# A polysketch attention and its expert router on one core: a new order for the steps ahead of the first expert block, and earlier waits at the close

## The chip, the core and the metric

The kernel runs on 1 core of a Trainium2 chip. The metric is the device time of one execution in microseconds (us): the runs shown of the kernel before are 196.06, 192.71 and 194.74 us, with a median of 194.74. All arithmetic on the matrix engine is in fp32, which the program writes as one matmul; the trace shows each such matmul as two or more passes, so counts of PE in the profile are larger than counts in the program.

## The reference

```python
# attention: 4 batches, 4 heads, 1088 rows, 32 columns, r = 8
def phi(x):
    a = np.einsum('rd,bhsd->bhsr', S1, x)
    b = np.einsum('rd,bhsd->bhsr', S2, x)
    return np.einsum('bhsi,bhsj->bhsij', a, b).reshape(*x.shape[:-1], r * r)
q_p, k_p = phi(q), phi(k)
kv = np.einsum('bhsf,bhsd->bhfd', k_p, v)
z = np.sum(k_p, axis=2)
num = np.einsum('bhsf,bhfd->bhsd', q_p, kv)
den = np.einsum('bhsf,bhf->bhs', q_p, z)[..., None] + 1e-06
x = (num / den)          # then heads side by side: 4352 rows of 128
# router: 8 experts, 128 -> 1024 -> 128
xn = x / (np.linalg.norm(x, axis=-1, keepdims=True) + 1e-06)
en = expert_emb / (np.linalg.norm(expert_emb, axis=-1, keepdims=True) + 1e-06)
logits = xn @ en.T / tau
expert_idx = np.argmax(logits, axis=1)
gate_w = softmax(logits)[np.arange(N), expert_idx]
for e in range(8):
    mask = expert_idx == e
    h = np.maximum(x[mask] @ w1[e], 0.0)
    out[mask] = gate_w[mask, None] * (h @ w2[e])
```

Every row goes through one expert alone, so the rows have to be sorted by expert before the two layers can run as full blocks.

## The kernel before, in words

**Two halves.** The four batches are worked on as two groups, `m = 0` and `m = 1`, of two batches each, and each group as five pieces: four of 4 tiles of 128 rows (called 0 to 3) and a rest (called r). For a piece, the keys go through these steps, which carry a name in the tables below (`keys`, L490): `ktr`, four transposes of 128x128 on PE, whose result ACT copies to `kT` (L426, L430); `kab`, the sketch with S1 and S2 together, PE's L447; `kb`, ACT's copy of the second factor (L453); `kp`, the product of the two factors on DVE or POOL (L463); `kv`, the sum of keys times values in PSUM (L529). In the first group a name has a 0 behind the kind (`ktr0 2`), in the second it has none (`ktr 2`). The queries of the first group take another way: `qtr` (L426), `pairs` (L611, 32 passes into two banks that hold both factors already spread), `sec` (ACT copies one factor, L620) and `prod` (DVE's product `held`, L623). Those of the second group go like the keys and are then turned: `trqp` (L641), `qpT` (ACT's copy, L647 or L650). When all keys and values of a group are in, `total` copies the sum to `kz`, `trkv` and `kvT` turn it (L544, L548), and `kve` and `kz` append its product with the experts' embeddings, `en_blk`. Then `nd` (L663) multiplies the queries' features with `kz`, which gives numerator, denominator and router logits at once, and `x` divides, so that the piece's rows and logits are in `xg`.

**Constants ahead of it.** `words` (L208) takes S1 and S2 apart on DVE, `sketches` (L229) turns them on PE (L231) into `Sblk` and `S_pairs`. The experts' embeddings go through `norm emb` (L359: square on ACT, power on POOL), `scale emb` (L367: DVE), `turn emb` (L382: PE's L385) and `place emb` (L387: DVE's `en_blk`). `lane`, `lanes`, `downs`, `positions` and `clear` make tables for the sorting. PE starts with matmuls on zeros that are used by nothing (L112, L115).

**The sorting of the first group.** `best 0`, `place 0`, `count`, `take 0`, `split 0`, `rest`, `mark`, `find`, `sums` and `tokens` find the best expert of each row, count rows by expert and make lists of rows; `exp0` also issues the first block's first layer, `weights(0)` (SP, L1080), whose expert SP reads from a register (L1073). `fetch` gathers a block's rows from DRAM by an indirect DMA of POOL's queue (L1046); `fetch0` is block 0's, `fetch 1` the next ones'. `turn 0` turns block 0's rows (PE's L1056, ACT's copy to `xTb`, L1058).

**The expert blocks.** 35 blocks of 128 rows follow. `up` is 16 passes (L1122) into `ps_big`, ACT's relu (L1130) makes `hT`, `down` is 16 passes (L1158) with the second layer in `w_sb`, and y goes out by an indirect DMA of POOL's queue (L1171). All second layers are loaded ahead of the blocks: six experts' on SP's queue after the keys, queries and values, and the last two in step `best 0` (L188). Group 1's other pieces of `nd` run between the first blocks. At the end SP drains and waits for the last nine first-layer loads (L1301 and L1302).

**What sets the order.** The program is recorded step by step, and each engine executes its instructions in the order of recording; nothing reorders them. Up to block 0 that order is two lists of step names written out by hand, `HEAD` (L399) and `ORDER` (L407). A step records its instructions for all of its engines at once, so a place in the list is a place on PE, ACT, DVE, POOL and the DMA queues of SP and ACT. From block 0 on, a table of times (`put_at`, `in_ticks`) sets the order.

```python
    for i, name in enumerate(x.strip() for x in HEAD.split(";")):
        put_at(0)(0, i, steps[name])
    ...
    for i, name in enumerate(x.strip() for x in ORDER.split(";")):
        put_at(4)(0, 47.2 + 0.01 * i, steps[name])
    put_at(first)(0, 32, lambda: weights(1))
    ...
            for i in sorted(at):
                for _, _, f in sorted(at[i], key=lambda x: x[:2]):
                    f()
```

Of the kernel before, what the change touches and what calls it, by code (L numbers as in the profile page):

```python
# [72 lines left out]
def kernel(  # L73
# [33 lines left out]
    nc.vector.memset(zeros, 0.0)  # L107
    ps_warm = ps_one("acc")

    def keep_warm(n):  # L110
        for _ in range(n):
            nc.tensor.matmul(ps_warm[:, :P], zeros[:, :P], zeros[:, :P], start=True, stop=True)  # L112

    for _ in range(7):
        nc.tensor.matmul(ps_warm[:2 * R, :2 * R], zeros[:, :2 * R], zeros[:, :2 * R], start=True, stop=True)  # L115
# [6 lines left out]
    for i, (s, queue) in enumerate(((S1, nc.sync), (S2, nc.scalar))):  # L122
        queue.dma_start(swords[i * R:(i + 1) * R].rearrange("p d w -> p (d w)"), s.bitcast(U32))
# [284 lines left out]
total0; kab 0 ab; trkv0; kvT0; ktr 1; kb 0; kve0; ktr 3; kz0; kp 0; nd 0 0; kab 1 acc; kb 1; ktr 2; x 0 0; nd 0 1; kp 1; kab 3 ab; kb 3;
kab 2 acc; kb 2; x 0 1; nd 0 2; trqp0r; ktr r; kp 3; kp 2; x 0 2; nd 0 3; kab r ab; kb r; kp r; x 0 3; qtr 1; qtr 0; kv 0; kv 1;
qab 0 t; qb 0; kv 3; best 0; place 0; count; qtr 3; qtr r; qp 0;  # L410
take 0; kv 2; kv r; qtr 2; trqp 0; total; split 0; trkv; qab 1 t; qab 3 ab; rest; mark 00; qb 1;
qab r ab; mark 01; find; exp0; kvT; qab 2 acc; sums; kve; qb 2; qpT 0; qb 3; qb r; qp 1; tokens; qp 3; kz;
trqp 1; nd 1 0; fetch0; fetch 1; qp 2; qp r; x 1 0; trqp 3; qpT 1; others; qpT 3; nd 1 1; x 1 1; trqp 2; norm 0; turn 0;
qpT 2; trqp r; qpT r"""
# [646 lines left out]

    def spread(i):

        squares[i] = tc.dram_tile([4, P // 4, 4, BLOCK], F32, name=f"squares{i}")
        nc.sync.dma_start(squares[i].rearrange("c b j a -> (b j) c a"), xs[i][:, :DM].rearrange("p (c a) -> p c a", c=4))

    def gather_squares(i):
        xq[i] = held[:, 0, i % 4 * P:(i % 4 + 1) * P]
        nc.sync.dma_start(xq[i], squares.pop(i).rearrange("c b j a -> (c b) (j a)"))
# [5 lines left out]

    loads = []
# [74 lines left out]

    def down(i):
# [12 lines left out]
        if i == USUAL - 1:  # L1165
            nc.vector.tensor_scalar_mul(y, ps, gate.pop(i)[:, 0:1])
        else:
            nc.scalar.activation(y, ps, ACT.Copy, scale=gate.pop(i)[:, 0:1])  # L1168
# [31 lines left out]
    def together(*fs):  # L1200
# [4 lines left out]
                  "best 0": together(steps["best 0"], steps["pick 0"], steps["write 0"], lambda: [load_w2(e) for e in (E - 2, E - 1)]),  # L1205
# [96 lines left out]
    for load in loads[-9:]:  # L1302
# [32 lines left out]
```

## Time and profile before

| what | number |
|---|---|
| three runs | 196.06, 192.71, 194.74 us |
| median | 194.74 us |
| the profiled execution | 194.15 us |
| its span from first to last instruction | 192.2 us |
| mean granted clock of PE | 0.994 |
| PE busy | 184.8 us (96%) in 2501 passes |
| weight loads beside it (PEld) | 175.4 us (91%) |
| DVE, ACT, POOL busy | 90.3, 98.7, 103.7 us |
| HBM read and written | 34.69 MB, 6.10 MB |
| block 0's first matmul | at 52.62 us |
| PE's last matmul ends | at about 187.5 us |

The span has three parts: the steps up to block 0 (0 to 52.62 us), the blocks (to 187.5 us), and the close (to 192.2 us). A row of the timeline or the chain gives the start in the span and the length; a releaser in brackets says which engine ended the wait ahead of the row. A row of the table by stages gives each engine's busy time in that stretch with the number of its instructions. Times lie within one profiled execution; the run's own time is 1.95 us longer than its span.

### The profile page before, as it was taken

To read this page: it belongs to the slowest core of one execution; us is meant where nothing else is said; L and a number is where in the kernel's file an instruction comes from. 1 tells how busy PE (TensorE), PEld (TensorE's weight loads), DVE (VectorE), ACT (ScalarE), POOL (GpSimd) and SP (SyncE) were. 2 spreads that over 40 slices of the span, in tenths; PEclk is the share of its full clock that TensorE was granted. 3 is DMA by queue.
4 is the path that set the end of the run, shared out by engine and by line. 5 is a ranking of instruction groups with operands and counts; after the bars stand their busy time and mean duration, and the time that the engine had idled before them with its cause. 6 is when DMAs were issued, how large, how long until landed. Compare 5 with 4: busy or idle time off the path is not lost.

```text
span 192.2 us, 6854 instructions
## 1 busy us (share of the span) xinstructions
PE 184.8 (96%) x2501; PEld 175.4 (91%) x2501; DVE 90.3 (47%) x396; ACT 98.7 (51%) x284; POOL 103.7 (54%) x134
## 2 busy tenths in 40 slices
PE   7999899999999999999999999999999999999990
PEld 7777788989889999999999999999999999999990
DVE  5789767789939578952232122122122121132200
ACT  3575353346572556534565555555555557657430
POOL 5110019302763765577877776776777775740532
PEclk9999999999999999999999999999999999999997
DMA  4999799998394987645558878788768998796000
GB/s 129 333 274 274 186 283 296 270 325 216 113 294 170 306 301 245 195 134 158 120 144 257 213 205 259 194 225 247 193 183 194 271 306 250 222 322 180 31 27 29
DMA packets 42596, 41.18 MB, mean 214 GB/s; under 512 B 17626, under 2 KB 36067, under 8 KB 42563
## 3 DMA queue, kind: packets, MB, share of 16 engines
q1 hardware_dynamic: 40272, 36.06, 64.7%
q0 software_dynamic: 2240, 4.67, 8.4%
q8 instruction: 21, 0.34, 0.8%
q14 instruction: 13, 0.10, 0.2%
q10 hardware_dynamic: 50, 0.01, 0.0%
HBM read 34.69 MB, written 6.10 MB: 212 GB/s over the span
## 4 chain that ended last, share of the span: by engine, by line
PE 70%; DMA 13%; issue 7%; POOL 4%; DVE 3%; ACT 1%; POOLq 1%; ACTq 0%
PE ps_big L1122 23%; DMA out_dram<-y,dst_i 13%; PE ps_acc L1158 11%; PE ps_ab L1158 10%; PE ps_big L663 6%; PE ps_acc L529 4%; PE ps_t L426 3%; POOL xs L1046 3%; PE ps_big L611 2%; PE ps_ab L447 2%; POOL norm L1136 2%; PE ps_acc L112 1%; PE ps_t L854 1%; PE ps_t L1056 1%; DVE row L778 1%
## 5 line engine op out<-in xcount | busy, mean ns | idle before, releaser
L1122 PE MATMUL ps_big<-xTb,wb 128*128 128x128 f32 x512 | 62.7, 276 | 0.4 <-PE ps_big L663 0.3
L1122 PEld LDWEIGHTS ps_big<-xTb,wb 128*128 128x128 f32 x512 | 59.7, 192 | 0.9 <-ACT sq L1135 0.4
L1171 POOL DMA_INDIRECT out_dram<-y,dst_i x35 | 35.9, 1027 | 40.5 <-ACT y L1168 17.6
L1130 ACT ACTIVATE hT<-ps_big 128x1024 f32<-128x1024 f32 x35 | 35.8, 1023 | 40.2 <-PE ps_big L1122 38.8
L1046 POOL DMA_INDIRECT xs<-rows,dst_i x35 | 35.6, 1018 | 18.4 <-DVE dst_i L871 11.4
L1158 PE MATMUL ps_ab<-w_sb,hT 128*128 x272 | 33.6, 276 | 0.0
L1158 PEld LDWEIGHTS ps_ab<-w_sb,hT 128*128 128x128 f32 x272 | 31.7, 192 | 0.2
L1158 PE MATMUL ps_acc<-w_sb,hT 128*128 x240 | 29.2, 275 | 0.0
L1149 DVE TENSOR_SCALAR gate<-gate 128x1 f32<-128x1 f32 x35 | 5.3, 150 | 50.3 <-ACT probs L1146 49.7
L1158 PEld LDWEIGHTS ps_acc<-w_sb,hT 128*128 128x128 f32 x240 | 28.0, 192 | 0.0
L1136 POOL TENSOR_TENSOR norm<-norm,half_c 128x1 f32<-128x1 f32 x35 | 21.7, 621 | 1.7 <-ACT sq L1135 1.3
L1053 DVE STREAM_TRANSPOSE xTb<-held 128x128 f32<-128x128 f32 x22 | 9.1, 413 | 13.6 <-DMA held<-squares 13.5
L463 POOL TENSOR_TENSOR kp<-both 128x1024 f32<-128x1024 f32 (+1 forms) x3 | 4.5, 1512 | 16.4 <-ACT both L458 16.4
L1168 ACT ACTIVATE y<-ps_ab,gate 128x128 f32<-128x128 f32 x17 | 6.2, 367 | 9.4 <-PE ps_ab L1158 9.4
L1146 ACT ACTIVATE probs<-xs,norm 128x8 f32<-128x8 f32 x35 | 10.4, 296 | 1.3 <-DVE norm L1139 1.3
L1168 ACT ACTIVATE y<-ps_acc,gate 128x128 f32<-128x128 f32 x17 | 6.2, 366 | 8.6 <-PE ps_acc L1158 6.8
L1135 ACT ACTIVATE sq<-xs 128x128 f32<-128x128 f32 x35 | 10.6, 302 | 0.1
L529 PE MATMUL ps_acc<-v,kp 128*64 128x64 f32 x224 | 7.8, 224 | 0.6 <-issue 0.6
L529 PEld LDWEIGHTS ps_acc<-v,kp 128*64 128x64 f32 x224 | 7.1, 138 | 1.4 <-issue 1.4
L430 ACT COPY qT<-ps_t 128x512 f32<-128x512 f32 (+1 forms) x10 | 5.1, 534 | 4.3 <-PE ps_t L426 4.3
L1127 PEld LDWEIGHTS ps_big<-xTb,wb 128*64 128x64 f32 x96 | 6.6, 137 | 0.5 <-DVE gate L1150 0.4
L1127 PE MATMUL ps_big<-xTb,v 128*64 128x96 f32 (+1 forms) x96 | 7.0, 249 | 0.0
(279 smaller groups left out, 280.8 us busy)
## 6 DMA issues: line engine op xcount, KB each, us to landing
wb<-in_moe_w_dram SPq DMA_DIRECT2D x35, 512.0 KB
w_sb<-in_moe_w_dram SPq DMA_DIRECT2D x16, 256.0 KB
rows<-xg SPq DMA_DIRECT2D x4, 544.0 KB
v<-in_v_dram SPq DMA_DIRECT2D x4, 512.0 KB
k<-in_k_dram SPq DMA_DIRECT2D x3, 512.0 KB
q<-in_q_dram SPq DMA_DIRECT2D x3, 512.0 KB
v<-in_moe_w_dram SPq DMA_DIRECT2D x3, 512.0 KB
squares<-xs SPq DMA_DIRECT2D x22, 64.0 KB
```

The lines of the kernel that those rows point to most:

```text
L529: nc.tensor.matmul(acc[m][u * HALF:(u + 1) * HALF, i, p], s["kp"][:, c - c0, h], bass.AP(tensor=vo.tensor, offset=vo.offset, ap=[list(vo.a ...
L663: nc.tensor.matmul(ps[i * HALF:(i + 1) * HALF, j * NEXT + p * W:j * NEXT + (p + 1) * W], q_[:, p, k_ * P + i * HALF:k_ * P + (i + 1) * HAL ...
L1046: nc.gpsimd.indirect_dma_start(out=xs[i][:], out_offset=None, in_=rows[:2 * S if t == 0 else N + 1], in_offset=bass.IndirectOffsetOnAxis(a ...
L1122: nc.tensor.matmul(ps[:, u, j * P:(j + 1) * P], w[:, f * P:(f + 1) * P], x, start=True, stop=True)
L1127: nc.tensor.matmul(ps[r, u, j * P + n0:j * P + n1], (w, first_b(i))[b][:, f * P + c * HALF:f * P + (c + 1) * HALF], x[:, n0:n1], start=Tru ...
L1130: nc.scalar.activation(hT[i], ps, ACT.Relu)
L1135: nc.scalar.activation(sq, xs[i][:, :DM], ACT.Square, accum_out=norms[i])
L1136: nc.gpsimd.tensor_tensor(out=norms[i], in0=norms[i], in1=half_c, op=ALU.pow)
L1146: nc.scalar.activation(p, xs[i][:, DM:], ACT.Exp, scale=norms.pop(i)[:, 0:1], accum_out=gate[i])
L1158: nc.tensor.matmul(ps, h[:, f * P:(f + 1) * P], ws[0][:, f], start=f == 0, stop=f == NF - 1)
L1168: nc.scalar.activation(y, ps, ACT.Copy, scale=gate.pop(i)[:, 0:1])
L1171: d = nc.gpsimd.indirect_dma_start(out=out[:, :], out_offset=bass.IndirectOffsetOnAxis(ap=dst_i[t][:, j:j + 1], axis=0), in_=y[:], in_offs ...
```

## The change

It does six things. (1) The two lists `HEAD` and `ORDER` are written in another order. All steps stay, and nine of them pass from the end of `HEAD` to `ORDER`. The first keys' transposes stand ahead of `norm emb` and `sketches`, and a new step `w2` appears. (2) The warm-up matmuls read the program's constant 0 instead of `zeros`, and there are 11 instead of 7 small ones. (3) S1 is loaded on ACT's queue, ahead of S2, and no longer on SP's. (4) The second layers of experts 6 and 7 are issued in `w2`, behind `weights(0)`, `find`, `sums` and `nd 1 0`, and no longer in `best 0`. (5) The list `loads` now also holds the DMAs of `spread` and `gather_squares` (L1066 and L1070 before). (6) The closing drain waits for the last 18 of `loads`, for the last block's last matmul and for the last two blocks' y, ahead of the waits that the program's end brings by itself.

```diff
@@ warm-up
+    nought = nc.const_aps.tensor(0.0, [P, P], F32)
...
-            nc.tensor.matmul(ps_warm[:, :P], zeros[:, :P], zeros[:, :P], start=True, stop=True)
-
-    for _ in range(7):
-        nc.tensor.matmul(ps_warm[:2 * R, :2 * R], zeros[:, :2 * R], zeros[:, :2 * R], start=True, stop=True)
+            nc.tensor.matmul(ps_warm[:, :P], nought, nought, start=True, stop=True)
+
+    for _ in range(11):
+        nc.tensor.matmul(ps_warm[:2 * R, :2 * R], nought[:, :2 * R], nought[:, :2 * R], start=True, stop=True)
...
-    for i, (s, queue) in enumerate(((S1, nc.sync), (S2, nc.scalar))):
+    for i, (s, queue) in enumerate(((S1, nc.scalar), (S2, nc.scalar))):
@@ HEAD
-constants; words; norm emb; one columns; clear 0; sketches; ktr0 0; qtr0 0; scale emb; kab0 0; kb0 0; turn emb; pairs 0; kp0 0;
-place emb; sec 0 0; ktr0 1; sec 0 1; qtr0 1; prod 0 0; prod 0 1;
...
+constants; words; ktr0 0; norm emb; clear 0; one columns; sketches; qtr0 0; ktr0 1; scale emb; kab0 0; turn emb;
+pairs 0; place emb; kb0 0; sec 0 0; sec 0 1; qtr0 1; kab0 1; kb0 1; ktr0 3; kp0 0; ktr0 2; pairs 1; prod 0 0;
...
@@ ORDER, its end
-trqp 1; nd 1 0; fetch0; fetch 1; qp 2; qp r; x 1 0; trqp 3; qpT 1; others; qpT 3; nd 1 1; x 1 1; trqp 2; norm 0; turn 0;
-qpT 2; trqp r; qpT r"""
+exp0; tokens; fetch0; qb 3; qb 2; trqp 1; qpT 1; nd 1 0; w2; qp 3; trqp 3; qb r; nd 1 1; qp 2; qp r; others; qpT 3;
+trqp r; turn 0; trqp 2; fetch 1; x 1 0; qpT 2; qpT r; x 1 1; norm 0"""
@@ steps
-                  "best 0": together(steps["best 0"], steps["pick 0"], steps["write 0"], lambda: [load_w2(e) for e in (E - 2, E - 1)]),
+                  "best 0": together(steps["best 0"], steps["pick 0"], steps["write 0"]),
+                  "w2": lambda: [load_w2(e) for e in (E - 2, E - 1)],
@@ the last blocks and the close
+        if i == USUAL - 1:
+            last.extend((made, y_made))
+        if i == USUAL - 2:
+            last.append(y_made)
...
     landed = nc.sync.drain()
-    for load in loads[-9:]:
+    for load in loads[-18:] + last:
```

Three places show how instructions move. First **PE at the program's start** (`k_` and `q_` are the first group's keys and queries, `emb_` the experts' embeddings). Before:

```order
L115 MATMUL ps_acc<-zeros 16x16 x7
L112 MATMUL ps_acc<-zeros 128x128 x6
L231 MATMUL ps_ab<-ident,srows 128x16
L426 MATMUL ps_t<-ident,k_117 128x128 x4
L426 MATMUL ps_t<-ident,q_118 128x128 x4
L447 MATMUL ps_ab<-Sblk,kT 64x4x16 x8
L385 MATMUL ps_acc<-ident,emb_304 128x8
L385 MATMUL ps_acc<-ident,emb_306 128x8
L611 MATMUL ps_big<-qT,S_pairs 64x256 x16
L426 MATMUL ps_t<-ident,k_117 128x128 x4
L426 MATMUL ps_t<-ident,q_118 128x128 x4
L447 MATMUL ps_ab<-Sblk,kT 64x4x16 x8
```

The same stretch of PE in the change:

```order
L116 MATMUL ps_acc<-const-float32-0.0 16x16 x11
L113 MATMUL ps_acc<-const-float32-0.0 128x128 x6
L426 MATMUL ps_t<-ident,k_121 128x128 x4
L232 MATMUL ps_ab<-ident,srows 128x16
L426 MATMUL ps_t<-ident,q_122 128x128 x4
L426 MATMUL ps_t<-ident,k_121 128x128 x4
L447 MATMUL ps_ab<-Sblk,kT 64x4x16 x8
L386 MATMUL ps_acc<-ident,emb_315 128x8
L386 MATMUL ps_acc<-ident,emb_317 128x8
L611 MATMUL ps_big<-qT,S_pairs 64x256 x16
L426 MATMUL ps_t<-ident,q_122 128x128 x4
L447 MATMUL ps_ab<-Sblk,kT 64x4x16 x8
```

The first keys' transposes now stand ahead of the sketches' one, and the second keys' transposes ahead of the first sketch of keys. The embeddings keep their place behind that sketch and ahead of the first `pairs`.

Second, **ACT at the program's start**, with the DMAs that it issues. Before:

```order
L123 DMA swords<-in_S_dram 8x64
L128 DMA emb_all<-in_moe_expert_emb_dram 8x128
L129 DMA tau_sb<-in_moe_tau_dram 8x1
L132 DMA rows<-zeros 1x136
L363 ACT_TABLE_LOAD
L363 ACTIVATE emb_sq,emb_ss<-emb_all 8x128
L430 COPY kT<-ps_t 128x256 x2
L430 COPY qT<-ps_t 128x512
L453 COPY kb<-ps_ab 128x128
```

In the change:

```order
L124 DMA swords<-in_S_dram 8x64 x2
L129 DMA emb_all<-in_moe_expert_emb_dram 8x128
L130 DMA tau_sb<-in_moe_tau_dram 8x1
L133 DMA rows<-zeros 1x136
L430 ACT_TABLE_LOAD
L430 COPY kT<-ps_t 128x256 x2
L364 ACTIVATE emb_sq,emb_ss<-emb_all 8x128
L430 COPY qT<-ps_t 128x512
L430 COPY kT<-ps_t 128x512
L453 COPY kb<-ps_ab 128x128
```

ACT has both halves of S to issue, and the square of the embeddings now stands behind the two copies of the first keys.

Third, **PE just ahead of block 0** (`kz_` is the second group's, `qp` and `qpT` its queries' features before and after the turn). Before:

```order
L641 MATMUL ps_big<-ident,qp 128x128 x8
L663 MATMUL ps_big<-kz_204,qpT 64x82 x16
L641 MATMUL ps_acc<-ident,qp 128x128 x4
L641 MATMUL ps_ab<-ident,qp 128x128 x4
L663 MATMUL ps_big<-kz_204,qpT 64x82 x16
L641 MATMUL ps_acc<-ident,qp 128x128 x4
L641 MATMUL ps_ab<-ident,qp 128x128 x4
L1056 MATMUL ps_t<-ident,xs 128x128
L641 MATMUL ps_t<-ident,qp 128x128 x2
L1073 TENSOR_LOAD exp_209
L1122 MATMUL ps_big<-xTb,wb 128x128 x8
```

In the change:

```order
L641 MATMUL ps_big<-ident,qp 128x128 x8
L663 MATMUL ps_big<-kz_208,qpT 64x82 x16
L641 MATMUL ps_acc<-ident,qp 128x128 x4
L641 MATMUL ps_ab<-ident,qp 128x128 x4
L663 MATMUL ps_big<-kz_208,qpT 64x82 x16
L641 MATMUL ps_t<-ident,qp 128x128 x2
L1056 MATMUL ps_t<-ident,xs 128x128
L641 MATMUL ps_acc<-ident,qp 128x128 x4
L641 MATMUL ps_ab<-ident,qp 128x128 x4
L1076 TENSOR_LOAD exp_213
L1123 MATMUL ps_big<-xTb,wb 128x128 x8
```

Eight transposes of the queries' features now stand between the turn of block 0's rows and block 0's first matmul, where two stood before.

More of the change, by code (lines that the diff above doesn't have):

```diff
@@ L405 @@
-positions; clear 1; ktr 0; kv0 2; kv0 3; kv0 r
+constants; words; ktr0 0; norm emb; clear 0; one columns; sketches; qtr0 0; ktr0 1; scale emb; kab0 0; turn emb;
+pairs 0; place emb; kb0 0; sec 0 0; sec 0 1; qtr0 1; kab0 1; kb0 1; ktr0 3; kp0 0; ktr0 2; pairs 1; prod 0 0;
+prod 0 1; sec 1 0; kp0 1; qtr0 2; kab0 2; lane; prod 1 0; sec 1 1; kb0 2; kv0 0; prod 1 1; qtr0 3; ktr0 r; kp0 2;
+pairs 2; sec 2 0; qtr0 r; sec 2 1; prod 2 0; prod 2 1; kv0 1; kab0 3; kb0 3; clear 1; kab0 r; qab0 r; downs; kp0 3;
@@ L406 @@
+ktr 0; kb0 r; qb0 r; pairs 3; kp0 r; sec 3 0
 """
     ORDER = """
[L408 to L411, printed above, removed]
@@ L412 @@
-qab r ab; mark 01; find; exp0; kvT; qab 2 acc; sums; kve; qb 2; qpT 0; qb 3; qb r; qp 1; tokens; qp 3; kz;
-trqp 1; nd 1 0; fetch0; fetch 1; qp 2; qp r; x 1 0; trqp 3; qpT 1; others; qpT 3; nd 1 1; x 1 1; trqp 2; norm 0; turn 0;
-qpT 2; trqp r; qpT r"""
+kv0 2; sec 3 1; lanes; prod 3 1; kv0 3; kv0 r; qp0 r; kab 0 ab; total0; trkv0; ktr 1; positions; kvT0; prod 3 0;
+kb 0; kve0; kz0; ktr 3; ktr 2; kp 0; nd 0 0; kab 1 acc; kb 1; nd 0 1; kab 3 ab; kab 2 acc; kb 2; kp 1; x 0 0; nd 0 2;
+kb 3; trqp0r; ktr r; nd 0 3; x 0 1; x 0 2; x 0 3; kab r ab; kb r; qtr 0; qtr 1; kp 3; kv 0; qab 0 t; kv 3; kv 1;
@@ L415 @@
+best 0; qb 0; qp 0; qtr r; place 0; kp 2; qtr 2; count; kp r; qtr 3; kv 2; kv r; trqp 0; total; take 0; split 0;
+trkv; rest; qab 1 t; kvT; mark 00; qab r ab; mark 01; qb 1; kve; kz; find; qp 1; qpT 0; qab 2 acc; qab 3 ab; sums;
+exp0; tokens; fetch0; qb 3; qb 2; trqp 1; qpT 1; nd 1 0; w2; qp 3; trqp 3; qb r; nd 1 1; qp 2; qp r; others; qpT 3;
+trqp r; turn 0; trqp 2; fetch 1; x 1 0; qpT 2; qpT r; x 1 1; norm 0"""
     AFTER_UP = ""
@@ L1060 @@
     squares, xq = {}, {}
+    loads = []
     def spread(i):
         squares[i] = tc.dram_tile([4, P // 4, 4, BLOCK], F32, name=f"squares{i}")
[L1065 removed]
+        loads.append(nc.sync.dma_start(squares[i].rearrange("c b j a -> (b j) c a"),
+                                       xs[i][:, :DM].rearrange("p (c a) -> p c a", c=4)))
     def gather_squares(i):
         xq[i] = held[:, 0, i % 4 * P:(i % 4 + 1) * P]
[L1069 removed]
+        loads.append(nc.sync.dma_start(xq[i], squares.pop(i).rearrange("c b j a -> (c b) (j a)")))
     def expert(t, j, engine):
@@ L1150, in share @@
         nc.vector.reciprocal(gate[i], gate[i])
+    last = []
     def down(i):
@@ L1157, in down @@
             if not two(i):
-                nc.tensor.matmul(ps, h[:, f * P:(f + 1) * P], ws[0][:, f], start=f == 0, stop=f == NF - 1)
+                made = nc.tensor.matmul(ps, h[:, f * P:(f + 1) * P], ws[0][:, f], start=f == 0, stop=f == NF - 1)
                 continue
@@ L1165, in down @@
         if i == USUAL - 1:
-            nc.vector.tensor_scalar_mul(y, ps, gate.pop(i)[:, 0:1])
+            y_made = nc.vector.tensor_scalar_mul(y, ps, gate.pop(i)[:, 0:1])
         else:
-            nc.scalar.activation(y, ps, ACT.Copy, scale=gate.pop(i)[:, 0:1])
+            y_made = nc.scalar.activation(y, ps, ACT.Copy, scale=gate.pop(i)[:, 0:1])
+        if i == USUAL - 1:
+            last.extend((made, y_made))
+        if i == USUAL - 2:
+            last.append(y_made)
         xs.pop(i)
```

4 lines of the change are left out of this document (removed).

## The prediction

> **What bounds the kernel now.** I read the page's first part, then a table by stages. I cut it at the first useful matmul, at the first `nd` (25.91), behind the last `nd` of the first half (34.36), at block 0 and where PE ends (below: from and to, length, busy time and count of PE, PEld, DVE, ACT and POOL, clock, DMA share, GB/s).
>
> ```profile
> PE 184.8 (96%) x2501; PEld 175.4 (91%) x2501; DVE 90.3 (47%) x396; ACT 98.7 (51%) x284; POOL 103.7 (54%) x134
> ```
>
> ```profile
> 4.62:25.91 21.29, 20.34 (x412) 15.70 (x412) 16.33 (x49) 11.99 (x32) 1.63 (x10) 1.00 0.98 267
> ...
> 34.36:52.62 18.26, 18.04 (x356) 16.22 (x354) 16.88 (x48) 8.73 (x25) 5.38 (x7) 1.00 0.77 231
> 52.62:187.50 134.88, 134.62 (x1514) 132.75 (x1514) 47.66 (x245) 73.47 (x219) 87.63 (x100) 1.00 0.71 208
> 187.50:192.20 4.70, 0.03 (x1) 0.00 (x0) 0.35 (x1) 0.00 (x0) 0.97 (x1) 0.73 0.09 30
> ```
>
> From 52.62 on PE is busy for 134.62 of 134.88 us. The change leaves the work and its order there alone, so that stretch costs the same and is only shifted by whatever moves the start of block 0. What is to be had lies in the 52.62 us ahead of it (the head) and the 4.70 us behind it. In the head PE is nearly full too, so I looked for its waits in the chain of waits (the row at 23.60 is the timeline's).
>
> ```profile
> 1.06 0.56 PE ps_acc L115 x14
> 9.33 0.69 PE ps_ab L447 x16
> 14.96 1.58 PE ps_big L611 x32
> 18.84 1.05 PE ps_big L611 x32
> 21.08 0.60 issue
> 23.60 0.69 PE L447 MATMUL ps_ab<-Sblk,kT 128*64 128x64 f32 x16
> 32.77 0.25 issue
> 52.62 2.05 PE ps_big L1122 x16
> ```
>
> One L611 group takes 1.58 where the next takes 1.05: 0.53 us lost. At 21.08 and 32.77 PE waits 0.60 and 0.25 us for nothing that the profile shows. All that a better order could win in one piece is of this size. PE lacks 0.95 us in the first row of stages and 0.22 in the second; that alone makes a change of 2% (3.9 us, about what a measurement of this kernel can tell from no change) unlikely.
>
> **The change, part by part.** *(a) The first ten microseconds.* PE's warm-up no longer needs DVE's `zeros`, so it can start some 0.3 us sooner, but has 8 more passes of 16x16 (0.56 us for 14, so 0.3): it ends as before, a little after 4. The first keys' copy takes S1's place on SP's queue and is issued at 0.74 instead of 1.20, so the keys are there by then, and their transposes no longer stand behind the sketches' one. What follows from it is on other engines (rows of the timeline):
>
> ```profile
> 1.20 0.41 SPq L142 DMA_DIRECT2D k<-in_k_dram  x1
> 4.62 0.99 PE L426 MATMUL ps_t<-ident,k 128*128 128x128 f32 x4
> 8.00 0.66 PE L426 MATMUL ps_t<-ident,k 128*128 128x128 f32 x4
> 3.68 0.31 ACT L363 ACTIVATE emb_sq<-emb_all 8x128 f32<-8x128 f32 x1
> 4.24 0.58 POOL L364 TENSOR_TENSOR emb_ss<-emb_ss,half_c 8x1 f32<-8x1 f32 x1 [1.43 <-ACT emb_sq L363]
> 5.28 0.13 DVE L369 TENSOR_SCALAR emb_ss<-emb_ss 8x1 f32<-8x1 f32 x1
> 5.65 0.65 ACT L430 COPY kT<-ps_t 128x256 f32<-128x256 f32 x2 [1.57 <-PE ps_t L426]
> 6.73 0.28 PE L385 MATMUL ps_acc<-ident,emb 8*128 8x8 f32 x2
> 7.14 1.23 DVE L463 TENSOR_TENSOR kp<-ps_ab,kb 128x1024 f32<-128x1024 f32 x1 [0.55 <-ACT kb L453]
> 8.29 0.28 DVE L389 TENSOR_TENSOR en_blk<-ps_acc,mask 128x32 f32<-128x32 f32 x2
> ```
>
> The table of the experts' embeddings is squared on ACT at 3.68 today, before ACT has anything else. In the change this stands behind the two `kT` copies, and those behind the key transposes, which run from 4.2 to 5.2 (0.99 a group at this point, where the same four take 0.66 later). Copies to 5.85, square and its read-out to 6.4 (0.56 from 3.68 to POOL's start), the power on POOL to 7.0, DVE's steps to the turn (5.28 to 6.73: 1.45): PE turns the embeddings at 8.5 instead of 6.73. By 7.2 PE has done the transposes, the sketch of the keys and even the second keys' transposes, and everything else on it stands behind the turn: a **new wait of about 1.2 us**. The DVE product `kp` now stands behind `en_blk`, so it runs from 9.1 to 10.4, and PE's second sketch of keys (L447 at 9.33 today), which needs its bank, starts at 10.5. Late by 1.2.
>
> S2 now goes second on ACT's queue. No row has that; the nearest are the first and second copies there and the DVE step that waits for both halves:
>
> ```profile
> 0.74 0.60 ACTq L123 DMA_DIRECT2D swords<-in_S_dram  x1
> 1.38 0.28 ACTq L128 DMA_DIRECT2D emb_all<-in_moe_expert_emb_dram  x1
> 2.47 0.21 DVE L213 TENSOR_SCALAR s_w<-swords 16x32 uint32<-16x32 uint32 x1
> 3.87 0.28 DVE L223 TENSOR_TENSOR srows<-srow,s_top 16x128 f32<-16x128 f32 x1
> ```
>
> Issued at 1.38 instead of 0.74, it lands between 0.64 us later and (as `emb_all`, which ACT uses at 3.68 where S2 is used at 2.47) 1.2 us later. So `srows`, ready at 4.15 today, is ready at 4.8 to 5.35, and the sketches' block at 6.4 at the latest, still ahead of the embeddings' turn: nothing more is lost at either end.
>
> *(b) To the end of the first keys and values.* The same PE work lies between the second sketch and the L447 at 23.60: 14.27 us today, of which 0.53 (L611) and 0.8 (the 0.60, and about 0.2 of passes that pause beside it) are waits. The change puts `kv0 0` and two more pieces ahead of that L611, so its 0.53 is covered: DVE has the product it waits for at 15.7, PE reaches it at 16.1. If the unexplained 0.8 stays away too, 12.9 us give 23.4: **ahead by 0.2**, that is 1.35 won against the 1.2.
>
> *(c) To the first `nd`.* DVE decides here, because its list starts late (`kp` ends at 10.4 instead of 8.37). Of the time from 8.37 to 24.58 the table by windows gives, beside DVE's longest wait and the end of that list:
>
> ```profile
> 8.37:24.58 16.21, 15.37 (x344) 12.01 (x343) 12.80 (x34) 9.52 (x25) 0.65 (x4) 1.00 0.98 255
> L623 DVE TENSOR_TENSOR held<-ps_big,qpT 128x512 f32<-128x512 f32 x8 | 5.3, 688 | 2.4 <-ACT qpT L620 2.4
> 24.58 0.29 DVE L548 COPY kvT<-ps_t 128x128 f32<-128x128 f32 x1 [0.80 <-PE ps_t L544]
> ```
>
> DVE is busy for 12.80 (the third figure behind the length). One `held` product (0.69) goes behind `kvT` in the change: 12.1, so 22.5 if it never waited. It waits 2.4 for ACT today; if all of that comes back `kvT` is at 24.9, if none does PE sets it at 24.4. I take the later: 0.3 late, of which the fourth keys' transposes, done by then, give back half: **0.15 lost**.
>
> *(d) To 52.62.* The unexplained 0.25 at 32.77 has a pause of like size beside it and no dependence that the new order has: **0.4 ahead** if it is chance. To 46.4 the same pieces change places; two groups of four transposes lose their neighbour:
>
> ```profile
> 12.07 0.60 PE L426 MATMUL ps_t<-ident,k 128*128 128x128 f32 x4
> 51.99 0.27 PE L1056 MATMUL ps_t<-ident,xs 128*128 128x128 f32 x1
> 52.30 0.27 ACT L1058 COPY xTb<-ps_t 128x128 f32<-128x128 f32 x1 [1.44 <-PE ps_t L1056]
> 46.76 1.21 POOL L1046 DMA_INDIRECT xs<-rows,dst_i  x1 [11.37 <-DVE dst_i L871]
> 46.01 8.62 SPq L1080 DMA_DIRECT2D wb<-in_moe_w_dram  x4
> ```
>
> A group behind another takes 0.60 (12.07), a lone one 0.66 (8.00): **0.1 lost** for two. Just ahead of block 0 the turned rows reach ACT at 52.30 and PE stands from 52.26 to 52.62. Now eight transposes (1.2 by the row at 12.07) lie between: **0.4 ahead**. The last two second layers (1024x128 of four bytes each, 1 MB) leave SP behind block 0's weights, issued at 46.01; PE does not wait for those today, so nothing is won there.
>
> Sum for the head: 1.2 late, 1.35 won, 0.15 lost, 0.4 won, 0.1 lost, 0.4 won: 0.7. I take half of the two waits without a cause (0.85) as coming back somewhere, since such waits are not tied to a step: 0.3 is left.
>
> *(e) The end.*
>
> ```profile
> 188.25 0.97 POOL L1171 DMA_INDIRECT out_dram<-y,dst_i  x1 [0.85 <-DVE y L1166]
> SPq L1330 <- DMA out_dram<-y,dst_i: 11.3, 4, 4.0
> 187.32 0.06 POOLq L1285
> ```
>
> The last copy out is issued until 189.22 and SP waits for it at the close, one of four such waits there (second row: their sum, count and longest). Those that are met long since are now taken sooner. No row prices such a wait; the nearest is a step of POOL's queue of 0.06, so four are 0.2. Below it is nothing (POOL's own close may end as late), above 0.3. I take 0.2, since SP's longest wait is the last DMA's.
>
> Together 0.5 us. The profiled execution took 194.15 us, its span 192.2 and 1.95 around it: 193.65. The three runs have a median of 194.74 and reach from 192.71 to 196.06; from their median it is 194.24. I forecast the middle, **193.9 us**.
>
> **Rivals.** *The head wins more*: the two waits without a cause stay away (0.4 more) and the embeddings' chain costs 0.4 instead of 1.2, because the keys' transposes run at 0.66 (0.8 more): 192.7. For it: each wait named above is loosened by the new order. Against: PE's order puts all pairs behind the turn of the embeddings.
>
> *Nothing comes out of it.* Both unexplained waits return in full and nothing is gained at the close: 0.7 less 0.85, 194.3 from the profiled execution, 194.9 from the median: 194.6. For it: they have no releaser, so no order removes them.
>
> *Slower: the late second layers meet block 0's rows.* The 1 MB used to be issued ahead of `wb`; now it moves from 47 on, at 231 GB/s (the row from 34.36) for 4.5 us, together with the 0.5 MB of `wb` and the rows that POOL gathers from 46.76 on. PE takes L1056 in order: if the first rows wait for all of it (52.0 instead of some time before 51.2), then the turn (0.27) and the eight transposes put block 0 at 53.3: 0.7 late instead of 0.3 ahead, 194.9 with the end as before. Against: the DMA share is 0.77 there, and the gathered rows are small. [...]
>
> *Slower: the pause puts PE back to its early rate.* At first a weight load is issued every 0.22 us, later one of the same shape every 0.12:
>
> ```profile
> 1.55 2.64 PEld L112 LDWEIGHTS ps_acc<-zeros 128*128 128x128 f32 x12
> 178.02 1.87 PEld L1122 LDWEIGHTS ps_big<-xTb,wb 128*128 128x128 f32 x16
> ```
>
> The change comes a little after 5, some 4.2 us after PE's start at 1.06. If the new wait of 1.2 us at 7.2 undoes it, the next 4.2 us of matmuls run at half rate again, 2.1 lost: 0.5 ahead becomes 1.6 behind, 195.8. Against: the L447 behind the 0.60 at 21.08 takes the same 0.69 as the one at 9.33. [...]
>
> **Numbers.** Forecast 0.38; wins more 0.20; nothing 0.24; second layers collide 0.12; half rate 0.06. The range 192.0 to 195.9 takes in all five and the runs' own spread of about 1.2 us to a side. The likeliest one alone: 193.0 to 194.8. Faster by over 2% would need all visible waits gone at once (0.05); slower by over 2% two of the slower cases together (0.04); within 2%: 0.91.
>
> **What would show it.** Right: PE's turn of the embeddings at 8 to 9 us with a wait ahead of it; the second sketch at about 10.5; the first L1122 at 52 to 52.8; no wait between L1056 and L1122; 134.9 us from there to PE's end; a close shorter by 0.2. Wrong: the embeddings turned before 7.5, or L1122 before 51.3 (the head wins more) or after 53 (look at when `xs` and `wb` land), or a stretch behind block 0 that isn't 134.9.

## The result, and the profile after

The change is slower. In 16 runs each, the median went from 193.94 to 196.18 us, ratio 1.0107 with a 95% interval of 1.0074 to 1.0140: some 2.1 us lost where 0.5 were forecast to be won, and the median lies above the range (192.0 to 195.9). A second comparison gave the same, 1.0104 (1.0065 to 1.0142). Here and below a ratio leaves out the executions more than 1.5% above the fastest of their kernel, and a median takes them all.

Two executions of the change were profiled: the first took 198.04 us, at the upper end of its runs, and the second (a_after in the experiments) 197.10, 0.8 above the median of its runs. I show the second for its rows and the first where it tells more. This is the chain of waits of the second one ahead of block 0 (start, length, what), and the table of what PE waited for up to 60 us (sum, times, longest):

```profile
47.24 0.19 DVE dst_i L871
47.43 0.29 issue
47.72 5.86 DMA xs<-rows,dst_i
53.58 0.14 issue
53.71 0.30 PE ps_t L1056
54.02 0.44 PE ps_acc L641 x4
54.45 0.44 PE ps_ab L641 x4
54.89 1.79 PE ps_big L1123 x16
```

```profile
PE ps_t L1056 <- DMA xs<-rows,dst_i: 1.6, 1, 1.6
...
PE ps_acc L529 <- issue: 0.7, 1, 0.7
PE ps_ab L232 <- DVE srows L224: 0.6, 1, 0.6
PE ps_big L1123 <- PE ps_big L663: 0.3, 1, 0.3
PE ps_big L663 <- issue: 0.2, 1, 0.2
```

Before, PE waited for the rows of block 0 not at all. Now the chain runs through their gather for 5.86 us, PE stands for 1.6 us ahead of L1056, and block 0 begins at 54.73 instead of 52.62. The small wait behind L1056 is gone, as forecast: its copy hides behind the eight transposes. The waits that the profile puts to "issue" are still there, on the same lines as before, L529 and L663.

The first profiled execution shows what a longer wait does (table by stages, columns as before):

```profile
52.00:54.00 2.00, 0.27 (x2) 0.03 (x1) 1.90 (x6) 0.00 (x0) 1.45 (x2) 1.00 1.12 309
54.00:56.00 2.00, 1.92 (x10) 1.95 (x11) 0.01 (x1) 0.85 (x2) 0.44 (x1) 0.57 1.07 354
56.00:60.00 4.00, 4.00 (x54) 3.83 (x54) 0.32 (x2) 2.44 (x8) 1.57 (x2) 0.79 0.86 318
```

PE stood from 52.27 to 54.05. Behind it the granted clock is 0.57 and 0.79: the trace has it at half from 54.3 to 57.7, into block 0. The rows landed at 53.95, 6.07 us after their issue, while DMA moved over 300 GB/s from 50 on. The half clock is not what makes the change slower in general: the mean granted clock is 0.987 in two of the sixteen executions (198.04 and 195.18 us) and 0.994 or more in the others.

The start and the close of the second execution (timeline; then the last stage from PE's end):

```profile
4.18 1.06 PE L426 MATMUL ps_t<-ident,k 128*128 128x128 f32 x4
5.81 0.29 PE L232 MATMUL ps_ab<-ident,srows 16*128 16x16 f32 x1 [0.57 <-DVE srows L224]
7.93 1.12 PE L447 MATMUL ps_ab<-Sblk,kT 128*64 128x64 f32 x16
8.98 0.38 PE L386 MATMUL ps_acc<-ident,emb 8*128 8x8 f32 x2
11.42 0.69 PE L447 MATMUL ps_ab<-Sblk,kT 128*64 128x64 f32 x16
```

```profile
190.65:195.03 4.38, 0.00 (x0) 0.00 (x0) 0.35 (x1) 0.00 (x0) 0.97 (x1) 0.96 0.12 36
```

The sketches' turn is at 5.81 (4.41 before), the embeddings' at 8.98, the second sketch at 11.42 (9.33 before). From PE's end to the end of the span it is 4.38 us; before it was 192.16 less 187.53, 4.63: the earlier waits at the close are worth 0.25. The second execution's span is 2.87 us longer than before's: block 0 begins 2.11 late, the stretch from there to PE's end takes 135.92 instead of 134.91, and the close gives 0.25 back. Of the 1.0 behind block 0, 0.75 is one more wait put to "issue", at 171.04 (last section).

### The profile page after: what moved, and what is told of

Read it like the earlier page. It is cut to its first block, busy times and chain, and to the rows that moved or that the text cites. A ratio compares the mean times of both kernels' runs of the same rounds, so it can differ in the third digit from the quotient of the medians.

```text
span 195.9 us, 6865 instructions
## 1 busy us (share of the span) xinstructions
PE 186.9 (95%) x2509; PEld 178.1 (91%) x2509; DVE 90.5 (46%) x396; ACT 99.2 (51%) x284; POOL 103.5 (53%) x134
## 4 chain that ended last, share of the span: by engine, by line
PE 78%; DMA 17%; issue 2%; DVE 1%; POOLq 1%; ACTq 0%; ACT 0%; DVEq 0%
PE ps_big L1123 26%; PE ps_ab L1161 13%; PE ps_acc L1161 13%; DMA out_dram<-y,dst_i 12%; PE ps_acc L529 5%; PE ps_t L426 4%; PE ps_big L663 4%; DMA xs<-rows,dst_i 3%; PE ps_big L611 2%; PE ps_ab L447 2%; PE ps_t L854 1%; DMA swords<-in_S_dram 1%; PE ps_big L1128 1%; PE ps_t L1056 1%; PE ps_acc L447 1%
## 5 line engine op out<-in xcount | busy, mean ns | idle before, releaser
L1123 PE MATMUL ps_big<-xTb,wb 128*128 128x128 f32 x512 | 63.5, 278 | 0.3 <-PE ps_big L663 0.3
L1123 PEld LDWEIGHTS ps_big<-xTb,wb 128*128 128x128 f32 x512 | 60.7, 195 | 0.6 <-ACT sq L1136 0.4
L1136 ACT ACTIVATE sq<-xs 128x128 f32<-128x128 f32 x35 | 10.5, 301 | 0.1
L529 PE MATMUL ps_acc<-v,kp 128*64 128x64 f32 x224 | 7.8, 223 | 1.1 <-issue 1.1
L529 PEld LDWEIGHTS ps_acc<-v,kp 128*64 128x64 f32 x224 | 7.1, 138 | 1.9 <-issue 1.8
L1140 DVE TENSOR_SCALAR norm<-norm 128x1 f32<-128x1 f32 x35 | 5.3, 152 | 5.3 <-POOL norm L1137 5.2
L430 ACT COPY kT<-ps_t 128x512 f32<-128x512 f32 (+2 forms) x10 | 4.7, 481 | 4.7 <-PE ps_t L426 2.6
```

The lines of the kernel that those rows point to most:

```text
L430: nc.scalar.copy(t[:, a:a + w], ps[:, a:a + w])
L529: nc.tensor.matmul(acc[m][u * HALF:(u + 1) * HALF, i, p], s["kp"][:, c - c0, h], bass.AP(tensor=vo.tensor, offset=vo.offset, ap=[list(vo.a ...
L1123: nc.tensor.matmul(ps[:, u, j * P:(j + 1) * P], w[:, f * P:(f + 1) * P], x, start=True, stop=True)
L1136: nc.scalar.activation(sq, xs[i][:, :DM], ACT.Square, accum_out=norms[i])
```

## The experiments

**Theories.** A: the last second layers (1 MB), issued behind block 0's weights, share the DMA engines with the gathered rows and hold them back. B: the start is the loss, because S2 comes late and PE's early rate lasts longer. F, formed from the first profiles: the two "issue" waits are PE waiting for its own instructions.

The kernels ran on five chips. On two of them, as in the first comparison, before takes 193.5 to 194.0 us (the quick chips below); on the other three 202.3 to 202.8, with its own runs spread over 4 to 7 us: there a per cent cannot be told, and the profiles say more than the times.

**First, a chip where before took 202.8.** e1 puts the second layers back, e2 puts S1 back on SP's queue, e5 does both, e3 moves only the second layers, in the kernel before.

```diff
# e1 and e5, from the change
-                  "best 0": together(steps["best 0"], steps["pick 0"], steps["write 0"]),
+                  "best 0": together(steps["best 0"], steps["pick 0"], steps["write 0"], lambda: [load_w2(e) for e in (E - 2, E - 1)]),
# e2 and e5, from the change
-    for i, (s, queue) in enumerate(((S1, nc.scalar), (S2, nc.scalar))):
+    for i, (s, queue) in enumerate(((S1, nc.sync), (S2, nc.scalar))):
# e3, from before (and best 0 without its loads)
-trqp 1; nd 1 0; fetch0; fetch 1; qp 2; ...
+trqp 1; nd 1 0; fetch0; w2; fetch 1; qp 2; ...
```

> The change with its last two second layers back in best 0, everything else as changed. Theory A (the second layers share the DMA engines with block 0's gathered rows): the rows take some 3 us from issue to landing again instead of 6.1, PE no longer stands from 51.9 to 54.0, its granted clock stays at 1.00 behind it, and 2 to 3.4 us come back: 193 to 194, ratio to before 0.995 to 1.002. Theory B (the late sketches at the start are the whole loss): the rows land as late as the fetch allows, and the time stays at 195.5 to 196.5, ratio about 1.010.

> The change with S1 back on SP's queue ahead of the first keys, everything else as changed. Theory B (S2 second on ACT's queue makes the sketches 1.5 us late, PE pauses from 4.4 to 5.7 and stays at its early rate until about 8.9): the sketches' turn at 4.3 instead of 5.7, the second sketch of keys at 9.5 to 10 instead of 11.2, block 0's fetch some 1 us sooner, 194.5 to 195.2, ratio 1.003 to 1.006. Theory A alone: the wait ahead of block 0 takes up what the start gains, and the time stays within 0.4 us of 196, ratio 1.008 to 1.011.

> Both undone: S1 on SP's queue, the last second layers in best 0; the two lists, the warm-up and the close as changed. If the two places are the whole loss and the prediction's other terms hold, 192.5 to 193.5, ratio 0.993 to 0.998. If the new order itself loses, no better than 194, ratio 1.000 or above.

> The kernel before with one thing changed: the last two second layers are issued behind block 0's weights and fetch, no longer in best 0. Theory A: the gathered rows land 2 to 3 us later than before (52 to 53 instead of 50), PE waits for them and falls back to its early rate, 1.5 to 3.5 us lost, ratio 1.008 to 1.018. Theory B: nothing that can be told, ratio 0.998 to 1.002.

Measured against before: e1 1.0004 (0.990 to 1.011), e2 1.0011 (0.994 to 1.008), e5 1.0027 (0.991 to 1.015), e3 1.0059 (0.999 to 1.013). No theory falls by these times. The profiles do tell something. With the second layers early (e1, e5) PE's L1056 waits for no rows; with them late (e2, e3) it does:

```profile
53.23 0.33 PE L1056 MATMUL ps_t<-ident,xs 128*128 128x128 f32 x1 [0.65 <-DMA xs<-rows,dst_i]
```

That is e3, the kernel before with the one step moved. In e2 the sketches' turn came at 4.76, but PE then stood for the second keys (1.24 us, released by the DMA of k at 6.87), because those keys are issued 0.4 us later when S1 goes first and PE comes to them sooner: the start's order and S1's place belong together. On this chip PE also waited 0.8 to 2.7 us for ACT's copy of the turned rows, which in e1 began 3 us after PE's turn had ended. ACT waited for PE's signal there: read from the trace, PE's signal for this turn comes 1.3 to 3.7 us after the recorded end of the turn in all twelve profiles from the three slower chips, and 0.01 to 0.02 us after it in all eight from the quick ones. What holds the signal back is not shown.

All six kernels profiled so far, before and the change included, had their "issue" wait at L529 exactly at PE's instruction 705 (weight loads, matmuls and PE's own waits counted), though different matmuls stand there. Before's other one, at 32.77, is at 1217, which is 705 and twice 256. So the next runs tested theory F beside A.

**Second, a chip where before took 194.0.** a_after is the change itself, a_w2_early is e1 again. f1 changes only the warm-up of the kernel before, f2 leaves out the load of six experts' second layers; their memory is filled with a constant, so those experts compute with other numbers.

```diff
# f1, from before
-    for _ in range(7):
+    for _ in range(39):
         nc.tensor.matmul(ps_warm[:2 * R, :2 * R], zeros[:, :2 * R], zeros[:, :2 * R], start=True, stop=True)
-    keep_warm(6)
# f2, from before; "blank" is recorded behind the step "lane"
-    for e in range(E - 2):
-        load_w2(e)
+    def blank_w2():
+        nc.gpsimd.memset(w2_sb[:, :E - 2], 0.01)
```

> The change itself, as a yardstick beside the two kernels that follow it on the same chip. If this chip's DMA is as quick as in the first comparison: 2 us over before, ratio 1.008 to 1.014. If it is a chip like that of the first four experiments (before at 202.8 us), no difference that can be told.

> The change with the last two second layers back in best 0, now beside the change on one chip. Theory A (they share the DMA engines with block 0's gathered rows): PE's turn of the rows waits for nothing, 1.5 to 3 us less than the change, ratio to before 0.995 to 1.003. Theory B (the start is the loss): within 0.5 us of the change.

> The kernel before with another warm-up of the same length: 39 small matmuls instead of 7, none of the six large ones, so that every later PE instruction stands 104 places further back in PE's stream (weight loads and matmuls counted alike). Theory F (the two waits without a cause are PE waiting for its own instructions, which come in pieces of 256): the wait of 0.6 us is again at PE's instruction 705 and the small one at 1217, which are now pieces of the program 104 instructions earlier (the sketch of the rest at L445 instead of the sums at L529), 1 to 3 us earlier in time. Rival (it belongs to the sums L529 or to their data): it stays at the same L529, now instruction 809.

> The kernel before without the loads of the first six experts' second layers (3 MB on SP's queue); POOL fills that memory with a constant instead, so the second layers of these experts compute with other numbers. Theory F (a piece of instructions waits on the DMA engines behind data): the traffic up to about 25 us is the same, so the wait at instruction 705 stays at 0.4 to 0.8; behind that the pieces come 1 to 2 us sooner after they are asked for than in before (3.3 us for the one that begins at 30.4), and the wait of 0.25 at instruction 1217 is gone. Rival (the pieces come at a pace of their own): 0.25 at 1217 as before.

Measured: a_after 1.0104 (1.0065 to 1.0142), a_w2_early 1.0034 (0.9994 to 1.0075), medians 196.29 and 194.68. These two kernels compared with each other differ by 1.5 us (ten executions each, 0.7 to 2.4): **most of the loss goes with the second layers' place** (theory A; the 0.3% that is left is not clear of the noise). The profile of a_w2_early shows the mechanism undone: the gather of block 0's rows, issued at 47.38, has landed at 51.18 (3.8 us, where a_after took 5.9 and before 3.4), and PE waits for nothing there. Over all profiles, as far as the trace has their landings, these rows take 4.7 to 6.1 us in the six with the late second layers and 2.9 to 4.6 in the fourteen with the early ones. Timeline of a_w2_early:

```profile
5.84 0.23 PE L232 MATMUL ps_ab<-ident,srows 16*128 16x16 f32 x1 [1.10 <-DVE srows L224]
8.30 0.36 PE L386 MATMUL ps_acc<-ident,emb 8*128 8x8 f32 x2 [0.44 <-DVE emb L380]
...
51.60 0.27 PE L1056 MATMUL ps_t<-ident,xs 128*128 128x128 f32 x1
...
52.58 1.95 PE L1123 MATMUL ps_big<-xTb,wb 128*128 128x128 f32 x16
```

f1 settles where the "issue" waits belong. The table by windows counts PE's and PEld's instructions up to a wait; first before up to its two waits, then a_after up to its first, then f1 up to its two:

```profile
0.00:21.09 21.09, 19.77 (x345) 15.33 (x346) 15.91 (x73) 11.72 (x29) 3.97 (x25) 1.00 0.93 258
0.00:32.78 32.78, 30.72 (x599) 25.15 (x600) 24.64 (x101) 16.50 (x41) 8.10 (x28) 1.00 0.93 253
```

```profile
0.00:22.28 22.28, 20.92 (x347) 16.51 (x348) 15.52 (x73) 11.69 (x28) 4.00 (x25) 1.00 0.94 257
```

```profile
0.00:24.42 24.42, 22.12 (x473) 17.61 (x473) 18.10 (x81) 12.47 (x31) 3.93 (x25) 1.00 0.88 239
0.00:32.46 32.46, 28.60 (x600) 23.25 (x601) 22.78 (x96) 15.53 (x38) 5.88 (x26) 1.00 0.94 253
```

345 and 346 are 691, 347 and 348 are 695, 473 twice is 946, 599 and 600 are 1199, 600 and 601 are 1201; PE's own waits make them 705, 961 and 1217: steps of 256. In f1 these numbers fall on other pieces of the program (the sketches L446, no longer the sums L529), and the waits went there: 1.42 us at 961 and 1.33 at 1217. My expectation named 705 and 1217 for f1; at 705 there was none, since PE came there late enough. So the waits stand at steps of 256 instructions, whatever the piece of the program; at which of them, depends on when the block arrives. Read from the trace, each block is one 16 KB packet on a DMA queue of its own, which starts after PE has entered the block ahead of it:

| kernel | PE enters the block ahead | packet | instruction | PE free, starts |
|---|---|---|---|---|
| before | 15.46 | 18.57 to 20.17 | 705 | 21.08, 21.68 |
| before | 27.14 | 30.41 to 31.59 | 1217 | 32.77, 33.02 |
| a_after | 17.13 | 20.33 to 21.45 | 705 | 22.27, 22.97 |
| a_w2_early | 27.39 | 30.89 to 32.10 | 1217 | 32.36, 33.37 |
| f1 | 19.67 | 22.55 to 23.89 | 961 | 24.41, 25.84 |
| f1 | 25.84 | 31.20 to 32.41 | 1217 | 32.45, 33.78 |

PE resumes 1.3 to 2.0 us after the packet's end; the packet begins 2.9 to 5.4 us after PE has entered the block ahead. f1 as a whole lost 2.7 us (1.0144, 1.0071 to 1.0216) with the same useful work: these two waits, and a warm-up of small matmuls that left PE at its early rate until about 9.6. f2 shows what the packet waits for. Its time (1.0280) means little, as POOL's fill of 5.2 us held up the start. But behind 24 us there is hardly any DMA traffic in it (DMA share and GB/s are the last two figures):

```profile
24.00:32.00 8.00, 7.87 (x200) 6.72 (x197) 6.54 (x21) 4.41 (x14) 0.00 (x0) 1.00 0.37 106
32.00:40.00 8.00, 8.00 (x190) 7.43 (x187) 6.41 (x19) 2.54 (x8) 5.94 (x4) 1.00 0.01 4
```

There the packets begin within 0.6 us of the entry (27.68 for 27.08, 32.81 for 32.55, 37.56 for 37.88), and PE waits at no block's start. My expectation for f2 held at 1217 and missed at 705, where I had named 0.4 to 0.8: PE came there 6 us later than in before, and the packet began 0.84 us after the entry. So a block of instructions waits behind data in the DMA engines; the rival, a pace of its own, falls.

**Third, two slower chips and a quick one.** Four kernels ran on two or three chips each (g, h and i are the chips): g1 is the change with the second layers early and the whole start as before; g2 is the kernel before with the change's start alone; g4 is the kernel before with the two gains that the profile shows, the transposes behind the turn and the close. g3 is e3 again.

```diff
# g1, from a_w2_early (and S1 on SP's queue, 7 small warm-up matmuls)
-constants; words; ktr0 0; norm emb; clear 0; one columns; sketches; qtr0 0; ktr0 1; scale emb; kab0 0; turn emb;
-pairs 0; place emb; kb0 0; sec 0 0; sec 0 1; qtr0 1; ...
+constants; words; norm emb; one columns; clear 0; sketches; ktr0 0; qtr0 0; scale emb; kab0 0; kb0 0; turn emb;
+pairs 0; place emb; sec 0 0; ktr0 1; sec 0 1; qtr0 1; ...
# g4, from before (and the close as in the change)
-... x 1 1; trqp 2; norm 0; turn 0;
-qpT 2; trqp r; qpT r"""
+... x 1 1; trqp r; turn 0; trqp 2;
+qpT 2; qpT r; norm 0"""
```

> The change with both suspects undone and the first ten microseconds as before: S1 on SP's queue, the embeddings squared first, sketches ahead of the keys' transposes, 7 small warm-up matmuls; the last second layers in best 0. What is left of the change is the order from the second keys on, the warm-up's source and the close. Theory F (PE's pace from 10 to 34 us is set by how its instructions come): the sketches' turn is at 4.4 instead of 5.8, and the 0.5 to 1 us that this gains carry through to block 0, 193.2 to 194.2, ratio 0.995 to 1.001. Rival (the start is taken up by the waits behind it): as the change with the second layers early, 1.002 to 1.005.

> The kernel before with the change's start alone: S1 and S2 on ACT's queue, the first keys' transposes ahead of the embeddings' square and of the sketches, the second keys' transposes ahead of the first sketch, the warm-up of 11 small matmuls on the constant. Theory F with the late sketches: the sketches' turn at 5.7, instruction 193 some 1 to 1.5 us late and instruction 705 as late as that, 0.8 to 1.5 us lost, ratio 1.004 to 1.008. Rival (the lateness is taken up by the wait at instruction 705): 0.999 to 1.002.

> The kernel before with the last two second layers behind block 0's weights and fetch, again, now on whichever chip has this call. Theory A: block 0's rows take 5 to 6.5 us from issue to landing, block 0 starts 1 to 2.5 us later than before, ratio 1.005 to 1.012. If the wait is there only when PE reaches the turn early (as in the change): within 0.3% of before.

> The kernel before with two things of the change that its profile shows as gains: eight transposes of the queries' features between the turn of block 0's rows and block 0, and the waits at the close taken sooner. The wait of 0.4 us ahead of block 0 and 0.25 us behind the last y go: 193.3 to 193.6 on a chip where before takes 194, ratio 0.997 to 0.999. If the rows' landing decides and not the copy: 0.999 to 1.001.

> The change with the last second layers early and the start as before (S1 on SP's queue, embeddings first, sketches first, 7 small warm-up matmuls). On a chip where before takes 194: if the start holds what is left of the loss, 193.2 to 194.0, ratio 0.995 to 1.000; if the order behind it holds it, 1.002 to 1.005.

> The kernel before with the change's start alone. If the late sketches and the longer stretch at PE's early rate carry through: 0.8 to 1.5 us lost, ratio 1.004 to 1.008. If PE's wait for its instructions at 21 us takes the lateness up: 0.999 to 1.002.

> The kernel before with the last two second layers behind block 0's weights and fetch. Theory A: the gathered rows land 2 to 3 us later, block 0 starts 1 to 2.5 us later, ratio 1.005 to 1.012. If the turn of the rows is late enough in this order to cover it: 0.999 to 1.002.

> The kernel before with eight transposes between the turn of block 0's rows and block 0, and the closing waits sooner: 0.4 and 0.25 us, 193.3 to 193.6 where before takes 194, ratio 0.996 to 0.999; if the landing of the rows decides and not their copy, 0.999 to 1.001.

> The change with the last second layers early and the start as before. Where before takes 194: if the changed start holds what is left of the loss, ratio 0.995 to 1.000; if the order behind it does, 1.002 to 1.005. Where before takes 202: 0.990 to 1.000 as in its two earlier runs.

> The kernel before with eight transposes between the turn of block 0's rows and block 0, and the closing waits sooner. Where before takes 194: 0.4 and 0.25 us, ratio 0.996 to 0.999; if the landing of the rows decides, 0.999 to 1.001. Where before takes 202: 0.985 to 0.995 as in its two earlier runs.

Measured on the two chips where before takes 202.4: the start alone 1.0066 (1.003 to 1.010) and 1.0041 (0.9996 to 1.009); the old start with the second layers early 0.990 and 0.995; the second layers moved alone 0.987 and 1.004, medians 0.8 us below and 0.75 above before; the two gains 0.979 and 0.985, medians 1.5 and 1.9 us below. With spreads of 4 to 6.7 us within these kernels I take from this only the sign for the start (late) and for the two gains (early), on such chips. The loss that theory A named for the second layers moved alone (1.005 to 1.012) did not show there: the rows took 4.7 and 5.3 us, but in g3 PE did not wait ahead of their turn, and in h3 0.9 us that the profile does not put to them. On a quick chip that kernel did not run.

On a chip where before takes 193.5 i2, the two gains, gave 1.0002 (0.9964 to 1.0040): nothing. Its profile says why. PE came to the turn of the rows at 50.43, 1.6 us earlier than before, and waited for the rows instead of for their copy. They landed at 51.48, 4.6 us after their issue (before 3.4); POOL's issue alone took 1.97 us instead of 1.20:

```profile
PE ps_t L1056 <- DMA xs<-rows,dst_i: 1.1, 1, 1.1
```

And i1 gave 1.0094 (1.0054 to 1.0135), more than either theory allowed: with the second layers early and the start as before the change still loses. So the parts do not simply add up. In its profiled execution the whole loss lies ahead of block 0, which begins at 54.84; from there to PE's end it takes 134.80. Its start is as quick as before's (instruction 193 at 8.83, before 8.81). At 14.82 PE stands 0.93 us for the rest of the keys, which this order uses earlier (g1 and h1, the same kernel, 0.8 and 2.2 us). Then it waits 2.47 us at instruction 705, for a packet that began 5.35 us after PE had entered the block ahead; behind that wait the granted clock fell (table by windows):

```profile
24.00:26.00 2.00, 2.00 (x55) 2.00 (x56) 0.18 (x4) 0.00 (x0) 0.00 (x0) 0.71 0.54 154
26.00:28.00 2.00, 2.00 (x35) 1.88 (x32) 0.00 (x0) 0.69 (x3) 0.00 (x0) 0.50 0.94 290
```

From 705 to 961 it took 7.14 us, where g1, the same kernel at full clock, took 5.62. That is one execution: the mean granted clock is 0.986 to 0.988 in five of i1's twelve and at least 0.997 in the other seven, whose median is 195.38 too. Where those seven lose is not shown; g1 waited 1.40 us at 705 and still ended the first half's `nd` at 34.29, as before did (34.32).

Over all profiled executions, nine with the new order wait at 705 in every one, 0.70 to 2.78 us, 1.38 on average; of nine with the old order, the shifted and the blanked kernel left out, four do not wait, and the mean is 0.59. Chance has a large share in each: seven of the nine have the same program as before up to there, and waited from 0 to 1.90 us.

On the quick chips the new order used up the block ahead in 5.1 to 5.3 us and the old one in 5.3 to 5.6, and the traffic until the packet began was 299 to 365 GB/s with the new order (four profiles), 277 and 275 with the old (two). The times of SP's loads do not explain this: the change's first execution issues group 1's second keys and values at 14.02 and 14.57, before at 15.28 and 15.80, but the three others with the new order on quick chips issue those keys at 14.84 to 15.09, and i1 has the longest wait at the lowest traffic of the four. What lengthens the packet's wait in the new order stays open. No version ran that beats both kernels where before takes 194.

## Why the prediction was wrong, step by step

**(a) The first ten microseconds: right in kind, S2 worse than its bound.** The new wait ahead of the embeddings came (0.44 us in a_w2_early; in a_after none, as PE was still at its early rate and so arrived late), the turn was at 8.30 and 8.98 (8.5 forecast), the second sketch at 10.22 and 11.42 (10.5). But S2 was used at 3.98 where I had bounded it by 2.47 and 1.2, 3.7; that the keys and queries, which SP now issues first, held it up was not tested apart. I had written that nothing more is lost there; the sketches' turn at 5.8 left PE idle for 0.5 to 1.1 us. In a_w2_early the two waits are 1.5 together, where 1.2 were forecast.

**(b) and (d), the waits without a cause: a step that failed in its reasoning.** I took them as chance "not tied to a step", counted them as won and then half of them as returning. They are tied to an instruction number (705 and 1217; 961 and 1217 in f1). The new order uses the block ahead up sooner (in 5.14 us in a_after, 17.13 to 22.27; before 5.62), and the next block's packet begins no sooner; what is won on the way is waited for there.

L611's 0.53 was indeed covered, and the wait at 705 did not stay away: 0.70 to 2.47 us on the quick chips, 0.60 before. From the second sketch to the one at 23.60 it took 13.7 us in both kernels (10.22 to 23.90 in a_w2_early, 11.42 to 25.07 in a_after), where 14.27 were to become 12.9: 0.6 won instead of 1.35, and the difference is the wait at 705 (0.76 and 0.70).

The first `nd` is at 26.55 in a_w2_early, 0.6 behind before; from there to block 0 it wins 0.65, close to the 0.7 forecast, although its wait at 1217 is 1.01 and not 0.25. So in that execution, without the late second layers, block 0 begins level with before (52.58, before 52.62), and not 0.3 ahead.

**(d), the second layers: the step that carries most of the miss.** I wrote that PE does not wait for block 0's weights today, "so nothing is won there", and put the edit at nothing. I had looked only at the loads that were moved and not at block 0's rows, which PE does wait for: the edit cost 1.5 us. The mechanism stood as a rival with a price of 1.0 (0.7 late instead of 0.3 ahead) and a chance of 0.12; the rows waited longer than its bound (53.6 to 54.0, not 52.0), for I took 231 GB/s over that 1 MB alone and left block 0's weights and the next blocks' rows out of the time. In a_after 255 GB/s were moved from the rows' issue to their landing, 1.5 MB in 6 us. (The rival's own sum is off as well: 52.0, 0.27 and 1.2 give 53.5 and not 53.3.) The sign of being wrong that I had named, block 0 after 53 and then the landing of `xs`, pointed to the right place.

Block 0's rows did not stand behind all of SP's loads: in a_after they landed at 53.58 and the last of the four second-layer loads at 55.97. But beside those loads they took 5.9 us there and 6.1 in the first execution, where they took 3.4 before and 3.8 in a_w2_early.

**The rival of half rate** was right in kind too, at another place: not the pause at 7.2 but the wait at 52 in the first execution and, in i1, the one at 21.4 were followed by half the clock (0.50 from 54.3 to 57.7, and 0.50 from 26 to 28). In a_after the 1.57 us wait at 52.1 was not (1.00 from 52 to 60). Its price was worked out from the profiled execution alone (195.8); from the base of the forecast it is 196.0, above the range.

**(d) the eight transposes and (e) the close: right.** The wait behind L1056 is gone, and the close is 0.25 shorter (0.2 forecast; over all profiles 4.34 to 4.58 us with the earlier waits, 4.55 to 4.84 without). i2 shows that the first is worth nothing by itself where the rows' landing is next in line. The stretch behind block 0 took 134.97 and 134.80 in a_w2_early and i1, as forecast (134.9), and 135.92 in a_after.

## What to carry to other kernels

Before a load is moved "behind" something, list every transfer that is on its way at the new place and which of them an engine waits for next: a load that nobody waits for still costs what it takes from the one that is waited for (here 1.5 us). An idle time that the profile puts to "issue" is worth counting instructions for: here it stood at the same count (705) in different orders and was PE's instruction supply, and a denser order only brought PE to it sooner. A gain read off one wait is real only up to the next thing in line, here the landing of the rows (i2: 1.0002 to before). And the length of a wait in one profile is one draw: the same program waited 0 to 1.90 us at the same instruction.

## What the runs showed of the hardware

PE's instructions came in blocks of 256 (the waits stand at 705, 961, 1217 and 4801), as 16 KB packets (before's page has 21 of them, 0.34 MB, on queue q8), about one block ahead (with the waits tabled above a packet began 2.9 to 5.4 us after PE had entered the block ahead), and a wait of 0.2 to 2.8 us arose where short matmuls used a block up in some 5 to 6 us while data filled the DMA engines (some 270 to 365 GB/s in the profiles above); even late in the kernel one did (a_after, instruction 4801, 193 and 18 times 256: 0.75 us from 171.04, behind passes of 32 to 96 columns that make the stream dense again).

The granted clock fell to half, for some 3.4 us (54.3 to 57.7 in the change's first execution) or twice that (f2: 0.58 on average from 8 to 16 us), behind some of PE's pauses, and the pause's length alone does not decide it. It fell after 1.78 us in the change's first execution, 2.47 in i1, 2.78 in e2 and 5.03 in f2, and after only 1.46 in e1, behind two short ones of 0.35 and 0.26; it did not after 1.57 in a_after and 2.16 in h4 (54.28 to 56.45). The end of the early rate varies from one execution to the next with the same start: four transposes at 4.14 took 0.60 us in a_w2_early, those at 4.18 took 1.06 in a_after, where the early rate lasted until about 10; the second sketch then came 1.2 us later.
